# Reading the moving operand of every MLP product in another order: pairs of four-element groups, taken in turn

## The chip, the cores and the metric

The kernel runs on one core of a Trainium2 chip. The metric is the device time of one execution in microseconds (us). Engines: PE is TensorE (matmuls; PEld is its weight load), DVE is VectorE, ACT is ScalarE, POOL is GpSimd, SP is SyncE, which issues most DMAs.

## What is computed

A chunked state-space scan over 4 sequences of 768 tokens and 8 heads, then two MLPs on its 3072 tokens of 256 features:

```python
x = attn_out.transpose(0, 2, 1, 3).reshape(B * S, H * D)      # 3072 x 256
xn = x / sqrt(mean(x * x) + 1e-06) * rms_g
x = (silu(xn @ w_gate) * (xn @ w_val)) @ w_out                # d_ff 1536
h = x @ w_in                                                  # d_ff 2048
out = softplus(h) @ w_out2
```

Nothing mixes tokens after the scan: each token goes through the norm and both MLPs by itself.

## The kernel before

Features lie on the 128 partitions and tokens along the free dimension. The tokens come in 24 units of 128; four units make a block of 512 tokens, and there are six blocks. A unit's scan runs on DVE (L561), its small matmuls on PE, and its norm on PE, DVE, ACT and POOL (L571 to L778). Each fp32 value that goes into an MLP product is split into a high and a low part of type fp32r (`xxh` and `xxl` for an input, `hw` for a hidden step, `..h` and `..l` for weights), and a product of two fp32 matrices is three matmuls: high by high, high weight by low input, low weight by high input.

For layer 1 a block runs 12 steps over the hidden features. A step's front, in `three_pass` (L791 to L797), makes two times six matmuls of 128 x 512 (weights `wg` and `wv`, two halves of the 256 features) into a PSUM tile `p`. ACT applies SiLU, DVE multiplies (L829), and ACT and DVE split the result into `hw` (L353, L360). The step's back (L868 to L873) adds six matmuls with `wo` into two tiles `t`. For layer 2 there are 16 steps with six matmuls of `wi` in front and six of `wp` behind. The two tiles `t` of a finished layer 1 are split again into `xxh` and `xxl` and are the input of layer 2; those of layer 2 are copied and stored to `out_y`, which is features by tokens, and the host transposes it. Every matmul goes through the helper `mm` (L322), so PE's rows in the profile all have line L322 and are told apart by their tiles.

At the start, matmuls of a constant by a constant keep PE busy until the first block is ready (the fillers, `p<-mean`: both operands are a single element, broadcast by a step of zero to 128 x 128 and 128 x 512).

The order of instructions on every engine is made before the launch by the class `Plan`. Each operation has a duration on its engine, a rank and its dependencies; the planner runs a list schedule on these and writes the instructions in the order found. Block 0's preparation has places written by hand. A product's duration and the due times of the steps are in units of `MM`, the time of one column, which stands in one line:

```python
    MM = 0.227 / 512
```

The weights come from HBM in 34 chunks (`wr`, L434) during the first third and are unpacked by two ACT and two DVE instructions each (L442 to L451), so the early blocks are calculated while weights are converted and later units are scanned.

Of the kernel before, what the change touches and what calls it, by code (L numbers as in the profile page):

```python
# [17 lines left out]
P = 128  # L18
NB, NH, SEQ, HD, NS = 4, 8, 768, 32, 16
DM = NH * HD  # L20
UPB = SEQ // P
# [38 lines left out]
KD = DM // P  # L60
# [229 lines left out]
def tile_ssd_then_swiglu_then_softplus_mlp(  # L290
# [17 lines left out]
    def buf(tag, shape, dt=F32, bufs=1):  # L308
        if bufs not in pools:
            pools[bufs] = ctx.enter_context(tc.tile_pool(name=f"sb{bufs}", bufs=bufs))  # L310
        return plan.buf(pools[bufs], bufs, tag, shape, dt)
# [5 lines left out]
    def pbuf(tag, shape):  # L317
        p, n = {"p": (ps_p, 4), "a": (ps_a, 2), "t": (ps_t, 2)}[tag]
        return plan.buf(p, n, tag, shape, F32)

    def mm(o, l, r, start, stop):
        pe.matmul(out=o, lhsT=l, rhs=r, start=start, stop=stop, skip_group_check=True)  # L322

    def f32(t):
        return t.bitcast(F32)

# [3 lines left out]
    def PE(ns, rank, fn, r=(), w=(), cols=0):  # L330
        plan.op({"pe": (ns, fn)}, rank, r, w, cols)
# [10 lines left out]
    def DVE(n, rank, fn, r=(), w=(), fast=False, port=True, ns=None):  # L342
        plan.op({"dve": (ns or dve_ns(n, fast), fn) + (("port",) if port else ())}, rank, r, w)
# [7 lines left out]
    def COPY(n, rank, out, in_, r, w, sbuf=True, on=("act",)):  # L351

        ways = {"act": (act_ns(n), lambda: act.activation(out=out(), in_=in_(), func=ACTF.Copy)),  # L353
                "dve": (dve_ns(n, sbuf), lambda: dve.tensor_copy(out(), in_())) + (("port",) if sbuf else ())}  # L354
        plan.op({e: ways[e] for e in on}, rank, r, w)

    def REST(n, rank, out, in_, hi, r, w, on=("dve",)):

        def fn(eng):
            return lambda: eng.tensor_tensor(out=out(), in0=in_(), in1=f32(hi()), op=ALU.subtract)  # L360
        ways = {"dve": (dve_ns(n), fn(dve), "port"), "pool": (pool_ns(n), fn(pool), "port")}
        plan.op({e: ways[e] for e in on}, rank, r, w)
# [31 lines left out]
        W[nm] = [const.tile([P, n, KD, P], F32R, name=f"{nm}{s}") for s in "hl"]  # L394


    MM = 0.227 / 512
    blocks, u0 = [], 0
    t_nom = T0
    for nu in BLOCKS:  # L400
        blocks.append(dict(u0=u0, nu=nu, n=nu * P, d1=18 * nu * P * MM, d2=12 * nu * P * MM))
        u0 += nu
# [5 lines left out]
    for layer, t in seq:  # L408
        b = blocks[t]
# [11 lines left out]
    def weight(c):  # L421
# [3 lines left out]
        if nm in ("wo", "wp"):  # L425
# [23 lines left out]
        ACT(n, rank, lambda: act.activation(out=h, in_=r(), func=ACTF.Copy, scale=256.0), [raw], [(nm, i, 0)])  # L449
        plan.now = first[3]  # L450
        DVE(n, rank, lambda: dve.scalar_tensor_tensor(out=l, in0=r(), scalar=256.0, in1=f32(h), op0=ALU.mult,  # L451
            op1=ALU.subtract), [raw, (nm, i, 0)], [(nm, i, 1)])
        plan.now = None
# [238 lines left out]
    def norm(t, o0, nu, rank, step, at):  # L692
# [6 lines left out]
        if t > 1:  # L699
# [9 lines left out]
            def msum():  # L709
                for k, p in enumerate((hi, lo)):  # L710
                    mm(nb()[:, 0:nu * P], mean.to_broadcast([P, P]).bitcast(F32R), p(), k == 0, k == 1)
            PE(2 * n * MM * 1e3, rank, msum, [hl, (hl, 1), "mean"], [nb], 2 * n)

# [74 lines left out]
    acc = {}  # L788
    x2 = {}

    def three_pass(o, wt, f, xh, xl, n):  # L791
        for k in range(KD):
            a = W[wt][0][:, f, k]
            b = W[wt][1][:, f, k]
            mm(o, a, xh[:, k, 0:n], k == 0, False)
            mm(o, a, xl[:, k, 0:n], False, False)
            mm(o, b, xh[:, k, 0:n], False, k == KD - 1)  # L797

    def wkeys(wt, f):
        return [(wt, f // 2, 0), (wt, f // 2, 1)]  # L800
# [12 lines left out]
    def front1(t, f, rank, new_table, early=False):  # L813
# [5 lines left out]
        for wt in ("wg", "wv"):  # L819
            gp = pbuf("p", [P, 4 * P])  # L820
            PE(6 * n * MM * 1e3, rank, lambda gp=gp, wt=wt: three_pass(gp()[:, 0:n], wt, f, xh(), xl(), n),
               xk + wkeys(wt, f), [gp], 6 * n)
# [10 lines left out]
    def front2(t, f, rank, new_table):  # L833
        bl = blocks[t]
        n = bl["n"]
        xh, xl = x2[t]
        hp = pbuf("p", [P, 4 * P])
        PE(6 * n * MM * 1e3, rank, lambda: three_pass(hp()[:, 0:n], "wi", f, xh(), xl(), n),
           [(x, m) for x in (xh, xl) for m in range(KD)] + wkeys("wi", f), [hp], 6 * n)
        s = buf("s", [P, 4 * P], F32, N_S)  # L840
        ACT(n, rank - EPI, lambda: act.activation(out=s()[:, 0:n], in_=hp()[:, 0:n], func=ACTF.Softplus), [hp],  # L841
            [s, "table"] if new_table and f == 0 else [s], 1283 if new_table and f == 0 else 0)
        if not (new_table and f == 0):
            plan.readers.setdefault("table", []).append(len(plan.ops) - 1)
        split_h((2, t, f), s, n, rank)

    def back(layer, t, f, rank):
        bl = blocks[t]
        n = bl["n"]
        nf, wt = ((F1, "wo"), (F2, "wp"))[layer - 1]  # L850
        if f == 0:
            acc[t] = [pbuf("t", [P, 4 * P]) for _ in range(KD)]
        hhl = H.pop((layer, t, f))

        end = (layer, t) == seq[-1] and f == nf - 1
        if end:

            def prods(p):
                for m in range(KD):
                    a, b = (W[wt][s][:, f, m] for s in (0, 1))  # L860
                    if p:
                        mm(acc[t][m]()[:, 0:n], a, hhl()[:, 1, 0:n], False, True)
                    else:
                        mm(acc[t][m]()[:, 0:n], a, hhl()[:, 0, 0:n], False, False)
                        mm(acc[t][m]()[:, 0:n], b, hhl()[:, 0, 0:n], False, False)
            for p in range(2):
                PE((4 - 2 * p) * n * MM * 1e3, rank, lambda p=p: prods(p), [hhl] + [(hhl, 1)] * p + wkeys(wt, f), list(acc[t]), (4 - 2 * p) * n)
        for m in range(0 if end else KD):  # L868
            def prod(m=m, o=acc[t][m]):
                a, b = (W[wt][s][:, f, m] for s in (0, 1))  # L870
                mm(o()[:, 0:n], a, hhl()[:, 0, 0:n], f == 0, False)
                mm(o()[:, 0:n], a, hhl()[:, 1, 0:n], False, False)
                mm(o()[:, 0:n], b, hhl()[:, 0, 0:n], False, f == nf - 1)  # L873
            PE(3 * n * MM * 1e3, rank, prod, [hhl, (hhl, 1)] + wkeys(wt, f), [acc[t][m]], 3 * n)
        if f < nf - 1:
            return
        if layer == 1:
            x2[t] = [buf(f"xx{k}", [P, KD, 4 * P], F32R, 3) for k in "hl"]
            for m in range(KD):
                h, l = ((lambda s=s, m=m: x2[t][s]()[:, m, 0:n]) for s in (0, 1))  # L880
                av = lambda a=acc[t][m]: a()[:, 0:n]
                COPY(n, rank - EPI, h, av, [acc[t][m]], [(x2[t][0], m)], False)
                DVE(n, rank - EPI, lambda h=h, l=l, av=av: dve.tensor_tensor(out=l(), in0=av(), in1=f32(h()), op=ALU.subtract),
                    [acc[t][m], (x2[t][0], m)], [(x2[t][1], m)], port=False)
        else:
            for m in range(KD):
                o = buf("s", [P, 4 * P], F32, N_S)
                COPY(n, rank - EPI, lambda o=o: o()[:, 0:n], lambda a=acc[t][m]: a()[:, 0:n], [acc[t][m]], [o], False,
                     ("dve",) if end and m else ("act",))
                c0 = bl["u0"] * P  # L890
                plan.op({"actq" if end and m else "sp": (1024, lambda o=o, m=m, q=act if end and m else nc.sync: q.dma_start(
                    out=out[m, :, c0:c0 + n], in_=o()[:, 0:n]))}, rank, [], [o])
# [117 lines left out]
def _launch(arrays):  # L1010
    import numpy as np
    import concourse.bacc as bacc
    from concourse.bass_utils import run_bass_kernel_spmd

    nc = bacc.Bacc("TRN2", target_bir_lowering=False, num_devices=1, dynamic_dma_scratch_size=1024)
    args, feed = [], {}
    for name, a in arrays.items():
        a = np.ascontiguousarray(a)
        feed[f"in_{name}"] = a
        args.append(nc.dram_tensor(f"in_{name}", a.shape, mybir.dt.from_np(a.dtype), kind="ExternalInput").ap())  # L1020
    args.append(nc.dram_tensor("out_y", (KD, P, NT), F32, kind="ExternalOutput").ap())
    with tile.TileContext(nc) as tc:
        tile_ssd_then_swiglu_then_softplus_mlp(tc, *args)
    return run_bass_kernel_spmd(nc, [feed], core_ids=[0]).results[0]["out_y"]
# [47 lines left out]
```

## Time and profile before

| | |
|---|---|
| median of 3 runs | 629.41 us (627.18 to 630.6) |
| the profiled execution | 629.57 us, of which its span is 627.8 us |
| PE busy | 622.6 us, 99% of the span |
| DVE busy | 351.9 us, 56% |
| ACT busy | 312.3 us, 50% |
| chain that ended last | 97% PE |

The span goes from the first to the last instruction of the program. The trace gives each instruction's start and duration. On PE a matmul starts before the one ahead of it has ended, so that durations overlap and their sum means little: how long one takes from the next is the difference of two start times, divided by the matmuls between. A group's line gives the busy time as the union of its instructions and the mean duration of one. Idle time before an instruction is put down to what released it.

### The profile page before, as it was taken

The numbers are of one execution on the slowest core, as the hardware profiler recorded it, in microseconds if no ns is written. First come the engines' busy times: TensorE is split into PE (matmuls) and PEld (weight loads), VectorE is DVE, ScalarE is ACT, GpSimd is POOL, SyncE is SP. The second block draws the span as 40 slices with busy tenths as digits, with TensorE's granted clock in tenths as the row PEclk, the third lists the DMA queues.
The fourth block names the chain that finished last, engine by engine and source line by source line (L and its number), as shares of the span: only waits on it lengthen the run. The fifth ranks groups of instructions, "written<-read, shape, count | busy, mean of one in ns | idle before, by whom it ended". The sixth has DMA issues, their size and how long they took to land.

```text
span 627.8 us, 8758 instructions
## 1 busy us (share of the span) xinstructions
PE 622.6 (99%) x3377; PEld 511.2 (81%) x3377; DVE 351.9 (56%) x561; ACT 312.3 (50%) x547; POOL 20.1 (3%) x41
## 2 busy tenths in 40 slices
PE   9999999999999999999999999999999999999997
PEld 7877788888888888888888888888888888888885
DVE  6999996788683236694333768645333433322222
ACT  2576665777555435444555344555423323643543
POOL 3310000000000000000000000000000000000000
PEclk9899999999999999999999999999999999999999
DMA  6667667576610014110346432400000000000000
GB/s 204 198 203 262 225 225 200 171 228 214 198 46 34 0 50 162 51 57 20 130 172 199 144 106 60 139 1 0 34 1 1 0 1 2 0 1 0 34 1 33
DMA packets 33433, 59.74 MB, mean 95 GB/s; under 512 B 3120, under 2 KB 14960, under 8 KB 33392
## 3 DMA queue, kind: packets, MB, share of 16 engines
q1 hardware_dynamic: 33248, 58.93, 28.7%
q8 instruction: 26, 0.43, 0.3%
q10 hardware_dynamic: 144, 0.26, 0.1%
q14 instruction: 15, 0.12, 0.1%
HBM read 47.45 MB, written 11.73 MB: 94 GB/s over the span
## 4 chain that ended last, share of the span: by engine, by line
PE 97%; DVE 1%; issue 0%; POOL 0%; ACT 0%; DVEq 0%; ACTq 0%
PE p L322 55%; PE t L322 37%; PE a L322 6%; DVE xxl L561 0%; DVE ab L610 0%; DVE xxh L561 0%; POOL xxl L360 0%; DVE xxl L610 0%; DVE xxh L610 0%; DVE s L354 0%; POOL rs L757 0%; DVE wr L445 0%; DVE xxl L778 0%; ACT xxh L353 0%; ACT wgh L449 0%
## 5 line engine op out<-in xcount | busy, mean ns | idle before, releaser
L360 DVE TENSOR_TENSOR hw<-s,hw 128x512 fp32r<-128x512 f32 x164 | 113.2, 691 | 158.1 <-ACT hw L353 157.3
L353 ACT ACTIVATE hw<-s 128x512 fp32r<-128x512 f32 x164 | 103.4, 632 | 103.6 <-DVE s L829 77.8
L322 PE MATMUL t<-hw,wph 128*128 128x512 f32 x384 | 118.9, 390 | 0.0
L841 ACT ACTIVATE s<-p 128x512 f32<-128x512 f32 x96 | 57.2, 598 | 88.2 <-PE p L322 84.6
L829 DVE TENSOR_TENSOR s<-s,p 128x512 f32<-128x512 f32 x72 | 49.4, 686 | 74.3 <-PE p L322 64.2
L322 PE MATMUL t<-hw,woh 128*128 128x512 f32 x272 | 84.6, 392 | 0.0
L322 PEld LDWEIGHTS t<-hw,wph 128*128 128x128 f32 x384 | 71.7, 188 | 15.6 <-ACT hw L353 0.4
L322 PE MATMUL p<-xxh,wih 128*128 128x512 f32 x192 | 75.0, 391 | 0.0
L322 PE MATMUL t<-hw,wpl 128*128 128x512 f32 x192 | 74.7, 389 | 0.0
L322 PE MATMUL p<-xxl,wih 128*128 128x512 f32 x192 | 74.7, 389 | 0.0
L322 PE MATMUL p<-xxh,wil 128*128 128x512 f32 x192 | 74.7, 389 | 0.0
L825 ACT ACTIVATE s<-p 128x512 f32<-128x512 f32 x72 | 43.0, 598 | 56.2 <-PE p L322 53.8
L322 PEld LDWEIGHTS t<-hw,woh 128*128 128x128 f32 x272 | 50.5, 188 | 11.1 <-issue 0.6
L322 PE MATMUL p<-xxh,wgh 128*128 128x512 f32 x144 | 56.5, 393 | 0.0
L322 PE MATMUL p<-xxh,wvh 128*128 128x512 f32 x144 | 56.3, 391 | 0.0
L322 PE MATMUL p<-xxl,wgh 128*128 128x512 f32 x144 | 56.2, 390 | 0.0
L322 PE MATMUL p<-xxl,wvh 128*128 128x512 f32 x144 | 56.1, 389 | 0.0
L322 PE MATMUL p<-xxh,wgl 128*128 128x512 f32 x144 | 56.1, 389 | 0.0
L322 PE MATMUL p<-xxh,wvl 128*128 128x512 f32 x144 | 56.1, 389 | 0.0
L322 PE MATMUL t<-hw,wol 128*128 128x512 f32 x136 | 53.0, 389 | 0.0
L561 DVE TENSOR_TENSOR_SCAN ab<-ab,ident 128x512 f32<-128x512 f32 x40 | 48.7, 1219 | 0.1
L322 PEld LDWEIGHTS p<-xxh,wih 128*128 128x128 f32 x192 | 36.0, 188 | 7.8 <-issue 0.4
(131 smaller groups left out, 751.7 us busy)
## 6 DMA issues: line engine op xcount, KB each, us to landing
wr<-in_w SPq DMA_DIRECT2D x34, 512.0 KB, 4.6
ab<-a_clip SPq DMA_DIRECT2D x20, 512.0 KB
parts<-wr SPq DMA_DIRECT2D x16, 512.0 KB
xc<-in_xc SPq DMA_DIRECT2D x20, 256.0 KB, 4.6
st<-parts SPq DMA_DIRECT2D x16, 256.0 KB, 4.4
cz<-parts SPq DMA_DIRECT2D x32, 128.0 KB, 2.8
out_y<-s SPq DMA_DIRECT2D x11, 256.0 KB, 3.6
wr<-in_bc SPq DMA_DIRECT2D x8, 256.0 KB, 3.0
```

Source lines behind the costliest of these rows:

```text
L322: pe.matmul(out=o, lhsT=l, rhs=r, start=start, stop=stop, skip_group_check=True)
L353: ways = {"act": (act_ns(n), lambda: act.activation(out=out(), in_=in_(), func=ACTF.Copy)), "dve": (dve_ns(n, sbuf), lambda: dve.tensor_co ...
L360: return lambda: eng.tensor_tensor(out=out(), in0=in_(), in1=f32(hi()), op=ALU.subtract)
L561: DVE(512, rank[0], lambda t=t, d=d: dve.tensor_tensor_scan(out=t(), data0=d(), data1=ident4, initial=0.0, op0=ALU.mult, op1=ALU.add), dk ...
L825: ACT(n, rank - EPI, lambda: act.activation(out=s()[:, 0:n], in_=ps[0]()[:, 0:n], func=ACTF.Silu), [ps[0]], [s, "table"] if new_table else ...
L829: DVE(n, rank - EPI, lambda: dve.tensor_tensor(out=s()[:, 0:n], in0=s()[:, 0:n], in1=ps[1]()[:, 0:n], op=ALU.mult), [s, ps[1]], [s], port= ...
L841: ACT(n, rank - EPI, lambda: act.activation(out=s()[:, 0:n], in_=hp()[:, 0:n], func=ACTF.Softplus), [hp], [s, "table"] if new_table and f ...
```

## The change

A function `swap` reorders the view of the moving operand, and all products of both MLPs read through it. The view cuts the 512 tokens into groups of eight, and each eight into two halves of four elements, and reads the halves in turn: elements 0, 4, 1, 5, 2, 6, 3, 7. The result of the product is written in the order of reading, so a product's output has its tokens exchanged within eight. A token goes through four such products (front and back of two layers); three exchanges give the order back, so the final output stands as after one, which the host undoes with a transpose. The weights, the outputs of the products and all other engines' views are as before.

```diff
+    def swap(t):
+        return t.rearrange("p (g l e) -> p g e l", l=2, e=4)
...
-    MM = 0.227 / 512
+    MM = 0.216 / 512
...
-            mm(o, a, xh[:, k, 0:n], k == 0, False)
-            mm(o, a, xl[:, k, 0:n], False, False)
-            mm(o, b, xh[:, k, 0:n], False, k == KD - 1)
+            mm(o, a, swap(xh[:, k, 0:n]), k == 0, False)
+            mm(o, a, swap(xl[:, k, 0:n]), False, False)
+            mm(o, b, swap(xh[:, k, 0:n]), False, k == KD - 1)
...
-                mm(o()[:, 0:n], a, hhl()[:, 0, 0:n], f == 0, False)
-                mm(o()[:, 0:n], a, hhl()[:, 1, 0:n], False, False)
-                mm(o()[:, 0:n], b, hhl()[:, 0, 0:n], False, f == nf - 1)
+                mm(o()[:, 0:n], a, swap(hhl()[:, 0, 0:n]), f == 0, False)
+                mm(o()[:, 0:n], a, swap(hhl()[:, 1, 0:n]), False, False)
+                mm(o()[:, 0:n], b, swap(hhl()[:, 0, 0:n]), False, f == nf - 1)
...
-    o = o.reshape(DM, UPB, NB, P).transpose(2, 1, 3, 0)
+    o = o.reshape(DM, UPB, NB, P // 8, 4, 2).transpose(2, 1, 3, 5, 4, 0)
```

The three products of the last back step (L861 to L866) are changed in the same way. Since `MM` sets the planner's durations and due times, the order of the instructions moves too. PE's is the same up to the 42nd product. There, in block 0, stand the small matmuls of a unit of block 1 (`a<-xc,Sm`, `a<-xc`, `a<-ab,xc`). Before:

```order
L322 MATMUL a<-xc,Sm 128x128 x2
L322 MATMUL a<-xc 32x64 x4
L322 MATMUL a<-ab,xc 32x128 x8
L322 MATMUL p<-xxh,wgh 128x512
L322 MATMUL p<-xxl,wgh 128x512
L322 MATMUL p<-xxh,wgl 128x512
L322 MATMUL p<-xxh,wgh 128x512
L322 MATMUL p<-xxl,wgh 128x512
L322 MATMUL p<-xxh,wgl 128x512
```

And after:

```order
L322 MATMUL p<-xxh,wgh 128x512
L322 MATMUL p<-xxl,wgh 128x512
L322 MATMUL p<-xxh,wgl 128x512
L322 MATMUL p<-xxh,wgh 128x512
L322 MATMUL p<-xxl,wgh 128x512
L322 MATMUL p<-xxh,wgl 128x512
L322 MATMUL a<-xc,Sm 128x128 x2
L322 MATMUL a<-xc 32x64 x4
L322 MATMUL a<-ab,xc 32x128 x8
```

The unit's matmuls stand six products later.

On PE, at the end of block 0, stands the matmul that broadcasts block 1's norm over the partitions (`a<-ident_68,rs`). Before, it has 180 products ahead of it, and the first product of block 1 is the 211th:

```order
L322 MATMUL a<-ident_68,rs 128x128 x4
L322 MATMUL p<-xxh,wvh 128x512
L322 MATMUL p<-xxl,wvh 128x512
L322 MATMUL p<-xxh,wvl 128x512
L322 MATMUL p<-xxh,wvh 128x512
L322 MATMUL p<-xxl,wvh 128x512
L322 MATMUL p<-xxh,wvl 128x512
L322 MATMUL t<-hw,woh 128x512 x2
L322 MATMUL t<-hw,wol 128x512
L322 MATMUL t<-hw,woh 128x512 x2
L322 MATMUL t<-hw,wol 128x512
```

And after, where it has 192 products ahead of it:

```order
L322 MATMUL p<-xxh,wvh 128x512
L322 MATMUL p<-xxl,wvh 128x512
L322 MATMUL p<-xxh,wvl 128x512
L322 MATMUL p<-xxh,wvh 128x512
L322 MATMUL p<-xxl,wvh 128x512
L322 MATMUL p<-xxh,wvl 128x512
L322 MATMUL t<-hw,woh 128x512 x2
L322 MATMUL t<-hw,wol 128x512
L322 MATMUL t<-hw,woh 128x512 x2
L322 MATMUL t<-hw,wol 128x512
L322 MATMUL a<-ident_68,rs 128x128 x4
```

The broadcast stands 12 products later, and the first product of block 1 is the 211th as before.

On DVE, behind the same norm: multiplies by the broadcast (`xxl<-xxl,a`), the low parts of the split (`xxl<-xxl,xxh`), and between them work on weights (`wol`), on hidden steps (`s`, `hw`) and on a later block's rows (`wr<-wr`). Before:

```order
L778 TENSOR_TENSOR xxl<-xxl,a 128x512
L451 SCALAR_TENSOR_TENSOR wol<-wr,woh 128x512
L829 TENSOR_TENSOR s<-s,p 128x512
L360 TENSOR_TENSOR xxl<-xxl,xxh 128x512
L778 TENSOR_TENSOR xxl<-xxl,a 128x512
L360 TENSOR_TENSOR hw<-s,hw 128x512
L482 TENSOR_TENSOR wr<-wr 128x512
L360 TENSOR_TENSOR xxl<-xxl,xxh 128x512
```

And after (the lines are five higher):

```order
L783 TENSOR_TENSOR xxl<-xxl,a 128x512 x2
L365 TENSOR_TENSOR hw<-s,hw 128x512
L365 TENSOR_TENSOR xxl<-xxl,xxh 128x512
L487 TENSOR_TENSOR wr<-wr 128x512
L834 TENSOR_TENSOR s<-s,p 128x512
L365 TENSOR_TENSOR xxl<-xxl,xxh 128x512
```

From the first multiply to the last split there were eight instructions, and there are seven now.

## Rows read from the trace of the kernel before

**Rows 1.** The page: busy time by engine, and the chain that ended last.

```profile
PE 622.6 (99%) x3377; PEld 511.2 (81%) x3377; DVE 351.9 (56%) x561; ACT 312.3 (50%) x547; POOL 20.1 (3%) x41
...
PE 97%; DVE 1%; issue 0%; POOL 0%; ACT 0%; DVEq 0%; ACTq 0%
```

**Rows 2.** Waits of PE: who waited for whom, total us, times, longest us.

```profile
PE p L322 <- DVE small L945: 0.9, 1, 0.9
PE p L322 <- POOL rs L757: 0.2, 1, 0.2
```

**Rows 3.** Timeline of PE at 304 us: start us, us, engine, instruction, count.

```profile
304.24 0.39 PE L322 MATMUL p<-xxh,wih 128*128 128x512 f32 x1
304.47 0.39 PE L322 MATMUL p<-xxl,wih 128*128 128x512 f32 x1
...
305.60 0.62 PE L322 MATMUL t<-hw,wph 128*128 128x512 f32 x2
306.05 0.39 PE L322 MATMUL t<-hw,wpl 128*128 128x512 f32 x1
...
308.32 0.39 PE L322 MATMUL p<-xxh,wih 128*128 128x512 f32 x1
```

**Rows 4.** Busy time in stretches: engines, granted clock, DMA share and GB/s.

```profile
core 0: us, PE busy (x) PEld busy (x) DVE busy (x) ACT busy (x) POOL busy (x), PEclk, DMA share, GB/s
8.20:10.30 2.10, 2.10 (x13) 1.88 (x12) 2.10 (x3) 0.00 (x0) 1.33 (x3) 1.00 0.89 254
28.00:29.30 1.30, 1.30 (x5) 1.03 (x4) 1.30 (x4) 0.66 (x2) 0.00 (x0) 0.50 0.20 39
30.00:90.00 60.00, 60.00 (x392) 47.61 (x391) 57.74 (x104) 38.54 (x74) 3.73 (x4) 1.00 0.66 223
260.00:280.00 20.00, 20.00 (x90) 16.50 (x89) 17.05 (x26) 9.37 (x18) 0.00 (x0) 1.00 0.19 69
460.00:580.00 120.00, 120.00 (x531) 99.34 (x531) 39.70 (x58) 45.57 (x74) 0.00 (x0) 1.00 0.00 1
```

**Rows 5.** A PE group of the page: instructions, busy us, mean ns, idle.

```profile
L322 PE MATMUL p<-xxh,wih 128*128 128x512 f32 x192 | 75.0, 391 | 0.0
```

**Rows 6.** Durations min/median/max ns: fillers from 8 us, products from 460 us.

```profile
L322 PEld LDWEIGHTS p<-mean x10: 187/188/191, 8.1 to 10.4; 128*128 128x128 f32 x10
L322 PE MATMUL p<-mean x9: 378/381/382, 8.2 to 10.4; 128*128 128x512 f32 x9
...
L322 PEld LDWEIGHTS t<-hw,wph x62: 187/188/188, 542.8 to 579.7; 128*128 128x128 f32 x62
L322 PE MATMUL t<-hw,wph x62: 389/389/389, 543.0 to 580.0; 128*128 128x512 f32 x62
```

**Rows 7.** Timeline of PE at 9 us, four fillers between unit matmuls.

```profile
9.34 1.03 PE L322 MATMUL p<-mean 128*128 128x512 f32 x4
10.21 0.40 PE L322 MATMUL p<-st,small 128*128 128x256 f32 x2
```

**Rows 8.** Timeline of PE at 28 us: three fillers, and the next.

```profile
27.81 1.49 PE L322 MATMUL p<-mean 128*128 128x512 f32 x3
...
29.09 0.63 PE L322 MATMUL p<-mean 128*128 128x512 f32 x1
```

**Rows 9.** Timelines of PE and DVE, 80 to 90 us: block 1's norm.

```profile
81.75 1.05 PE L322 MATMUL a<-ident,rs 128*128 128x128 f32 x8
82.56 0.48 PE L322 MATMUL p<-xxh,wvh 128*128 128x512 f32 x1
...
89.48 0.39 PE L322 MATMUL p<-xxh,wgh 128*128 128x512 f32 x1
...
83.02 0.68 DVE L778 TENSOR_TENSOR xxl<-xxl,a 128x512 f32<-128x512 f32 x1
...
87.24 0.69 DVE L360 TENSOR_TENSOR xxl<-xxl,xxh 128x512 fp32r<-128x512 f32 x1
```

More of the change, by code (lines that the diff above doesn't have):

```diff
@@ L861, in prods @@
                     if p:
-                        mm(acc[t][m]()[:, 0:n], a, hhl()[:, 1, 0:n], False, True)
+                        mm(acc[t][m]()[:, 0:n], a, swap(hhl()[:, 1, 0:n]), False, True)
                     else:
-                        mm(acc[t][m]()[:, 0:n], a, hhl()[:, 0, 0:n], False, False)
-                        mm(acc[t][m]()[:, 0:n], b, hhl()[:, 0, 0:n], False, False)
+                        mm(acc[t][m]()[:, 0:n], a, swap(hhl()[:, 0, 0:n]), False, False)
+                        mm(acc[t][m]()[:, 0:n], b, swap(hhl()[:, 0, 0:n]), False, False)
             for p in range(2):
```

## The prediction

> **What bounds the kernel now.** I first read the share of busy time and the chain that ended last: TensorE (PE) has 622.6 us of a span of 627.8, and 97% of the chain is PE [rows 1]. A busy PE alone does not say that PE is the bound, because the ends of its matmuls are modelled, so I looked next at what PE waited for: 0.9 us at the start and 0.2 us once, nothing else [rows 2]. So from the first product to the last PE runs from one matmul to the next, and what sets the time is the pace of those matmuls.
>
> The pace is read from the start times, not from the durations, which overlap. Between 304.24 and 308.32 us stand 18 products (the 6 of one `wi` step, then 12 of two pairs of `wp` steps): 4.08 us / 18 = 226.7 ns each [rows 3]. The stretch from 460 to 580 us confirms it over a longer way: 531 matmuls touch 120 us, two of which began before, so 120 / 529 = 226.8 ns [rows 4]. There are 6 blocks of 12 x 18 + 16 x 12 products, 2448 in all, of which the group of the `wi` products shows its 6 x 16 x 2 = 192 [rows 5]. 2448 x 226.7 ns = 555 us: the change touches 88% of the span.
>
> Why 226.7? [...] Other engines and DMA: from 460 to 580 us DMA moves 1 GB/s and VectorE (DVE) is busy a third of the time, and the pace is no better than at 304 us, where weights and units still come in [rows 3, 4]. The weight load: 188 ns for a product's and 188 ns for a filler's, alike [rows 6]. The moving operand: the fillers at the head are matmuls of the same shape and type whose moving operand is one element read 512 times, and four of them take 10.21 - 9.34 = 0.87 us, 217.5 ns each, while DVE is busy throughout and DMA moves 254 GB/s [rows 4, 7]. Their median duration is shorter by the same kind of step, 381 against 389 ns [rows 6]. So what a product pays over a filler, about 9 ns, goes with walking through 512 elements, and that walk is the one thing that the change alters in each product.
>
> [...]
>
> **The change part by part.** *The new read order* (all 2448 products). It adds and removes no instruction. Within each eight neighbours the columns go in as 0, 4, 1, 5, 2, 6, 3, 7, so each group of four is still used up once and within eight columns. [...] No effect: 226.7 ns, nothing. A loss: the rivals below have it. [...] The filler shows what a product costs when the walk is free, so I take a value between the floor and the filler, 216 ns: 2448 x (226.7 - 216) = 26.2 us. With the filler's 217.5 it would be 22.5 us.
>
> [...]
>
> *The planner's constant.* `MM` goes from 0.227 to 0.216 per 512 columns, so due times move and the order on every engine changes; the numbers of instructions on PE, DVE, ScalarE (ACT), POOL and the load queue stay the same, and up to the 42nd product so does PE's order. It is an input, and says nothing on the chip. Its cost sits where another engine has no room. From 30 to 90 us DVE is busy 57.74 of 60 us [rows 4], and in it lies the norm of block 1, whose result the first product of block 1 (the 211th in program order) reads. Before: broadcast on PE at 81.75, multiplies from 83.02, last split at 87.24 + 0.69 = 87.93, first use at 89.48 [rows 9]; that is 6.18 us of chain and 1.55 us to spare. After: the broadcast stands 12 products later, with 18 products left to the first use. These and the broadcast itself (82.56 - 81.75 = 0.81 us) last 18 x 0.216 + 0.81 = 4.7 us. If the chain takes 6.18 us as before, PE waits 1.5 us; with one DVE instruction fewer between first multiply and last split (about 0.6 us), 0.8 us. If DVE paces all of block 0, PE wins nothing on its 210 products, 210 x 10.7 ns = 2.2 us lost; if the cover holds, 0. I take 1.2 us. The next fullest place, 260 to 280 us, has DVE at 17.05 of 20 us [rows 4], and 17.05 / 19.1 still leaves a tenth free: nothing.
>
> *The output's order* is set right on the host by a transpose of the result, outside the time. The output of each product is still written to consecutive places, and ACT, DVE and the DMAs see the same shapes as before: nothing.
>
> **Sum.** The profiled execution took 629.57 us, of which 627.8 are span; the median of the runs is 629.41, the same within 0.03%. 629.57 - 26.2 + 1.2 = 604.6 us.
>
> **The rivals.** (a) *The walk costs by bytes, whatever the order.* [...] Against it: nothing in the rows but that today's reads leave one group of four and need the next at once, which the new order spreads. Then only the plan changes, 629.6 to 631 us with the wait of 0 to 1.5 us at block 1.
>
> (b) *Slower: each change of group is paid.* The old order leaves a group of four 127 times in a product, the new one 511 times. [...]
> [...]
>
> (c) *Half the gain.* The extra cycles fall only in part, to some 221 ns: 2448 x 5.7 ns = 14 us, less the 1.2, 616.8 us.
>
> **How the numbers follow.** Forecast, products at the pace of a free walk: 0.74, with its own range from 597 (floor, no wait) to 610 us (filler's pace and 2.2 us lost). (c), 610 to 622: 0.08. (a), 627 to 631: 0.08. (b), 700 and up: 0.10. A measurement of this kernel tells about 0.5%, 3 us, from no change. Faster by more than that are the forecast and (c), 0.82; within it (a), 0.08; slower (b), 0.10. The forecast and (c) hold 0.82, so the range goes from 597 to 620 us, and the other two stay outside.
>
> **What would show it.** In the trace after, 18 products between the same places should take 3.89 us in place of 4.08, in the quiet stretch after 440 us as well as in the busy one; the duration recorded of one should fall from 389 toward 381 ns, and the weight loads stay at 188. PE should show a wait of about a microsecond on DVE or ACT at the 211th product and next to none elsewhere, DVE should be as long busy as now, 352 us, in a shorter span. I am wrong if products keep 226.7 ns (a), if they take 260 ns and more (b), or if the pace falls but PE's waits in the first 100 us exceed 2.2 us.

## The result, and the profile after

The changed kernel took 603.77 us (median of 4 runs, 601.38 to 604.33) beside 629.5 us before: ratio 0.9589, 95% interval 0.9551 to 0.9626. The prediction was 604.6 us. The profiled execution took 604.33 us with a span of 601.3 us. A row of the profile after whose line number is five higher than before is the same code, since `swap` added five lines.

Busy time by engine and the chain that ended last, of the kernel after (beside [rows 1]), and PE's waits (beside [rows 2]):

```profile
PE 595.0 (99%) x3377; PEld 513.7 (85%) x3377; DVE 351.2 (58%) x561; ACT 309.5 (51%) x547; POOL 20.0 (3%) x41
...
PE 94%; DVE 3%; DMA 1%; issue 0%; ACT 0%; POOL 0%; DVEq 0%; ACTq 0%
```

```profile
PE p L322 <- DVE small L950: 0.9, 1, 0.9
PE t L322 <- DVE hw L365: 0.9, 2, 0.7
PE p L322 <- POOL rs L762: 0.2, 1, 0.2
```

The other engines do what they did: DVE 351.2 us after 351.9, ACT 309.5 after 312.3. PE still has the chain, and its waits grew by 0.9 us of idle time. The pace is read as in [rows 3], on PE's timeline between two like places (start us, us, instruction, count):

```profile
291.46 0.38 PE L322 MATMUL p<-xxh,wih 128*128 128x512 f32 x1
291.68 0.38 PE L322 MATMUL p<-xxl,wih 128*128 128x512 f32 x1
...
292.76 0.59 PE L322 MATMUL t<-hw,wph 128*128 128x512 f32 x2
...
295.35 0.38 PE L322 MATMUL p<-xxh,wih 128*128 128x512 f32 x1
```

18 products take 3.89 us, 216.1 ns each, where they took 4.08. In the quiet stretch of the kernel after, where DMA moves almost nothing (columns as in [rows 4]), with the durations (min/median/max ns) of its weight loads and products beside those of [rows 6]:

```profile
435.00:555.00 120.00, 120.00 (x557) 105.08 (x557) 41.74 (x61) 47.54 (x78) 0.00 (x0) 1.00 0.00 1
...
L322 PEld LDWEIGHTS t<-hw,wph x60: 189/189/189, 520.1 to 553.3; 128*128 128x128 f32 x60
L322 PE MATMUL t<-hw,wph x60: 379/379/379, 520.3 to 553.5; 128*128 128x512 f32 x60
```

557 matmuls touch 120 us, two of them begun before: 216.2 ns. The duration fell from 389 to 379 ns, the weight load stayed. All of the 2448 products that follow one another undisturbed go at this pace; over all start times the median is 216 ns, and the mean of the undisturbed ones is 215.8.

Where the 26.5 us of span come from: the first product starts at 30.03 us (30.51 before), and from there to the end it is 571.27 us (597.29 before), 26.0 us less. 2448 x (226.7 - 215.8) ns is 26.7 us. That the sum comes out lower has two parts of opposite sign, which are taken up below: new waits, and products just behind other matmuls that no longer lose time.

### The profile page after: what moved, and what is told of

The parts are those of the page before. It is cut to its first block, busy times and chain, and to the rows that moved or that the text cites. A ratio compares the mean times of both kernels' runs of the same rounds, so it can differ in the third digit from the quotient of the medians.

```text
span 601.3 us, 8773 instructions
## 1 busy us (share of the span) xinstructions
PE 595.0 (99%) x3377; PEld 513.7 (85%) x3377; DVE 351.2 (58%) x561; ACT 309.5 (51%) x547; POOL 20.0 (3%) x41
## 4 chain that ended last, share of the span: by engine, by line
PE 94%; DVE 3%; DMA 1%; issue 0%; ACT 0%; POOL 0%; DVEq 0%; ACTq 0%
PE p L322 53%; PE t L322 35%; PE a L322 6%; DMA wr<-in_w 1%; DVE hw L365 1%; DVE wr L450 0%; DVE s L834 0%; DVE ab L566 0%; DVE xxl L783 0%; POOL xxl L365 0%; DVE xc L730 0%; DVE xxl L615 0%; DVE wol L456 0%; DVE s L359 0%; DVE wvl L456 0%
## 5 line engine op out<-in xcount | busy, mean ns | idle before, releaser
L322 PE MATMUL t<-hw,wph 128*128 128x512 f32 x384 | 114.7, 380 | 0.1
L322 PE MATMUL t<-hw,woh 128*128 128x512 f32 x272 | 82.3, 383 | 1.0 <-DVE hw L365 0.9
L322 PE MATMUL p<-xxh,wih 128*128 128x512 f32 x192 | 72.8, 379 | 0.0
L322 PE MATMUL p<-xxl,wih 128*128 128x512 f32 x192 | 72.8, 379 | 0.0
L322 PE MATMUL p<-xxh,wil 128*128 128x512 f32 x192 | 72.8, 379 | 0.0
L322 PE MATMUL t<-hw,wpl 128*128 128x512 f32 x192 | 72.8, 379 | 0.0
L322 PE MATMUL p<-xxh,wgh 128*128 128x512 f32 x144 | 55.0, 382 | 0.0
L322 PE MATMUL p<-xxh,wvl 128*128 128x512 f32 x144 | 54.6, 379 | 0.0
L322 PE MATMUL p<-xxl,wgh 128*128 128x512 f32 x144 | 54.6, 379 | 0.0
L322 PEld LDWEIGHTS p<-xxh,wil 128*128 128x128 f32 x192 | 36.3, 189 | 5.1
```

## The experiments

Where kernels are compared closely, the time from the first product to the end is taken, which is called the rest below. It leaves out the start, which varies by itself, as the last section shows.

**The order and the plan apart.** The first kernel keeps the new order and has the old constant, the second has the new constant alone.

```diff
-    MM = 0.216 / 512      # e1_order_old_plan: the changed kernel, but
+    MM = 0.227 / 512
...
-    MM = 0.227 / 512      # e2_new_plan_only: the kernel before, but
+    MM = 0.216 / 512
```

> The new read order with the planner's old constant 0.227, so that the order of instructions is nearly that of before. If the read order alone makes the gain: 18 products in 3.88 us (215.8 ns each), duration 379 ns, about 602 to 606 us; PE's waits in the first 100 us may differ from the 0.4 us of the changed kernel. If the plan carried part of the gain: over 610 us.

> The planner's new constant 0.216 alone, products read in the old order. If the read order alone makes the gain: 226.7 ns a product, 629 to 632 us, no difference that can be measured. If the plan carried part of it: under 626 us.

The order alone: 600.92 us, ratio 0.9558 (0.9528 to 0.9587). The plan alone: 628.75 us, ratio 1.0009 (0.9991 to 1.0027), the same. The quiet stretches of the first and of the second show 215.8 and 226.8 ns (120 us by 556 and 529):

```profile
440.00:560.00 120.00, 120.00 (x558) 105.08 (x557) 40.56 (x60) 49.93 (x83) 0.00 (x0) 1.00 0.01 5
...
460.00:580.00 120.00, 120.00 (x531) 99.41 (x530) 39.67 (x58) 45.57 (x74) 0.00 (x0) 1.00 0.00 1
```

The gain is the order's alone. The rest says what the plan does: 597.29 us before and 598.53 with the new constant; 571.27 us after and 570.47 with the old one. In these profiles the new constant costs about 1 us either way.

**Whose walk costs: the weights' or the moving operand's?** The expectations count in a cycle that is the author's estimate: the 426.7 ns of a filler at a granted 0.50 ([rows 4, 8]), halved for 1.00, are 213.3 ns, a 512th of that is called a cycle, and the 226.7 ns of a product are 32 of these more than 213.3. No run shows such a cycle, or a product at 213.3 ns: the fastest pace of any run is 215.8. A weight load reads 128 elements, which are 32 groups of four as well; so the weight load that runs beside each product was a candidate that its 188 ns in [rows 6] do not rule out. Two kernels replace one of the operands by a single element per partition, as the fillers have both.

```diff
-            a = W[wt][0][:, f, k]                            # e3_flat_weights (all products alike)
+            a = W[wt][0][:, f, k, 0:1].to_broadcast([P, P])
...
     def swap(t):                                             # e4_flat_moving (old constant)
-        return t.rearrange("p (g l e) -> p g e l", l=2, e=4)
+        return t[:, 0:1].to_broadcast([P, 4 * P])
```

> The kernel before with the weights of every product replaced by one of their columns, broadcast, so that a weight load reads one element 128 times; the moving operand is read in the old order. This changes the output. A weight load has 128 elements, 32 groups of four, and the product has 32 cycles too many. If each group of a weight load takes a cycle from the moving read: 216 ns a product, about 603 us. If the moving operand's walk alone costs: 226.7 ns still, about 629 us.

> The kernel before with the moving operand of every product replaced by its first column, broadcast, as the fillers have it; the weights are read as before. This changes the output. If the moving operand's walk costs the 32 cycles: 215.5 to 217.5 ns a product, about 603 us. If the weight load's walk costs them: 226.7 ns and 629 us.

Flat weights, then flat moving operand, quiet stretches:

```profile
460.00:580.00 120.00, 120.00 (x520) 97.82 (x519) 38.78 (x57) 44.41 (x73) 0.00 (x0) 1.00 0.00 1
...
440.00:560.00 120.00, 120.00 (x557) 105.05 (x556) 40.78 (x60) 49.85 (x82) 0.00 (x0) 1.00 0.01 5
```

With a flat moving operand a product takes 216.2 ns (120 us by 555), and the kernel 601.4 us: the walk of the moving operand is the cost, and the new order is as good as no walk at all. With flat weights it is not 216 ns, and not 226.7 either but 231.7 (120 us by 518; 635.37 us). This fits neither of the two outcomes that were expected. So the weight load does not cause what a product takes beyond 216 ns, as e4 shows with the weights read as before, but where it reads does bear on the walk, with 231.7 ns for 226.7; why is open.

The changed kernel has a control of its own. The sums of the norm (`a<-ab,mean`) have the same shape and type, broadcast weights as in e3, and still read their operand in running order. PE's timeline of the kernel after:

```profile
161.90 0.38 PE L322 MATMUL t<-hw,wpl 128*128 128x512 f32 x1
162.12 0.63 PE L322 MATMUL a<-ab,mean 128*128 128x512 f32 x2
162.58 0.59 PE L322 MATMUL t<-hw,wph 128*128 128x512 f32 x2
163.01 0.38 PE L322 MATMUL t<-hw,wpl 128*128 128x512 f32 x1
```

Two of them take 0.46 us, 230 ns each and close to the 231.7 ns of e3, in the midst of products at 0.43 us for two.

**What in the order does it?** Six kernels are the changed one with another `l` and `e` in `swap` (and the host's inverse of it). Each alters all 2448 products and ran once. e5 has a view of the same form as the change, with other numbers in it.

```diff
-        return t.rearrange("p (g l e) -> p g e l", l=2, e=4)     # 0 4 1 5 2 6 3 7
+        return t.rearrange("p (g l e) -> p g e l", l=2, e=2)     # e5_within_group: 0 2 1 3
+        return t.rearrange("p (g l e) -> p g e l", l=4, e=4)     # e6_four_groups: 0 4 8 12 1 5 9 13
+        return t.rearrange("p (g l e) -> p g e l", l=2, e=8)     # e7_groups_apart: 0 8 1 9 2 10
+        return t.rearrange("p (g l e) -> p g e l", l=128, e=4)   # e8_new_group_each: 0 4 8 12 16
+        return t.rearrange("p (g l e) -> p g e l", l=2, e=256)   # e9_halves_apart: 0 256 1 257
+        return t.rearrange("p (g l e) -> p g e l", l=4, e=2)     # e10_two_at_a_time: 0 2 4 6 1 3 5 7
```

> The changed kernel with pairs of two in place of four (columns 0, 2, 1, 3): the order is new, but each group of four is still read to its end before the next. If what helps is to take two groups of four in turn: 226.7 ns a product, about 629 us. If any order other than the running one helps: 216 ns, about 603 us.

> The changed kernel with four groups of four in turn (0, 4, 8, 12, 1, 5, ...). If the read can hold two groups only and pays each change beyond them: over 226.7 ns, up to 267 ns (728 us). If taking groups in turn is free as such: 215.8 ns, about 603 us.

> The changed kernel with two runs of eight in turn (0, 8, 1, 9, ... 7, 15): two groups are held at a time as in the change, but they are not neighbours. If two groups in turn suffice: 215.8 ns, about 603 us. If they must be neighbours: 226.7 ns, about 629 us.

> The changed kernel with all 128 groups of four in turn (0, 4, 8, ..., 508, 1, 5, ...): each read goes to another group, and none is used again before 128 columns. [...] If each change of group that was not read shortly before is paid with a cycle or more, up to one column in two cycles: 267 to 427 ns a product, 728 to 1120 us. If not even that is paid: 215.8 to 226.7 ns, 603 to 629 us.

> The changed kernel with the two halves of the operand in turn (0, 256, 1, 257, ...): two groups of four at a time, 1024 bytes apart. If two groups in turn are free wherever they lie: 215.8 ns a product and 571 to 572 us from the first product to the end. If they must lie close together: over 226.7 ns, up to the 268 ns of four groups in turn.

The expectation of the sixth kernel describes its order wrongly: it is 0, 2, 4, 6, 1, 3, 5, 7, two reads of one group and two of the next, but the two are not neighbours.

> The changed kernel with two neighbouring elements at a time of two groups in turn (0, 1, 4, 5 written the other way round: 0, 2, 4, 6, 1, 3, 5, 7), so each group is read twice, left for two columns, and read twice again. If what helps is that a new group is needed some columns after the group before it was opened, and not four in a row from one: 215.8 ns. If the group must change at each column: 226.7 ns.

Quiet stretches of 120 us in the order e5, e7, e9, e6, e10, e8:

```profile
460.00:580.00 120.00, 120.00 (x531) 99.36 (x530) 39.02 (x57) 46.00 (x75) 0.00 (x0) 1.00 0.00 1
...
440.00:560.00 120.00, 120.00 (x557) 105.08 (x557) 40.88 (x60) 49.86 (x82) 0.00 (x0) 1.00 0.01 5
...
440.00:560.00 120.00, 120.00 (x558) 105.08 (x557) 41.50 (x61) 47.86 (x78) 0.00 (x0) 1.00 0.00 1
...
560.00:680.00 120.00, 120.00 (x448) 84.92 (x447) 32.79 (x48) 42.52 (x70) 0.00 (x0) 1.00 0.01 5
...
700.00:820.00 120.00, 120.00 (x354) 69.54 (x353) 25.39 (x37) 31.72 (x51) 0.00 (x0) 1.00 0.00 0
...
1000.00:1120.00 120.00, 120.00 (x261) 54.18 (x260) 17.12 (x25) 29.00 (x47) 0.00 (x0) 1.00 0.01 5
```

In all six PE is busy for the whole stretch, the granted clock is 1.00 and DMA still; only the count of matmuls differs. With the pace from start times and each kernel's time:

| order of reading | ns a product | us | reads in a row from one group, by every second column |
|---|---|---|---|
| one element only (e4) | 216 | 601.4 | all |
| 0 4 1 5 2 6 3 7 (the change) | 216 | 603.8 | 4 |
| 0 8 1 9 2 10 (e7) | 216 | 602.8 | 4 |
| 0 256 1 257 (e9) | 216 | 608.4 | 4 |
| 0 1 2 3 (before) | 226.7 | 629.5 | 2 |
| 0 2 1 3 (e5) | 227 | 628.5 | 2 |
| 0 4 8 12 1 5 9 13 (e6) | 268 | 730.6 | 1 |
| 0 2 4 6 1 3 5 7 (e10) | 340 | 903.7 | 1 |
| 0 4 8 12 16 (e8) | 461 | 1198.4 | 1 |

e8 and e10 are dearer than any outcome that was expected of them (up to 427 and 226.7 ns). Three explanations fall. That any order but the running one helps, or the form of the view as such: e5 shows no gain. That groups must be neighbours: e7 and e9 go at the same pace, with elements eight and 256 places apart in turn. That the read keeps the last two groups, whichever column asks: then e10, which never has more than two groups in use, would be cheap, and it costs 340 ns. What fits all nine is the count in the last column. Number the columns in the order of reading, take columns 0, 2, 4, ... by themselves and columns 1, 3, 5, ... by themselves, and count how many in a row come from one group of four. Where it is four or more, a product took 216 ns; where it is two, 226.7 and 227; where it is one, 268 to 461. The count was formed on these rows and no further run tested it; what in the read makes it so, no run shows. It does not say why the three orders with single reads differ among themselves, nor why flat weights made the running order dearer.

The halves (e9) are a warning beside it. The pace is the same, yet the rest took 576.1 us for 571.3. In this execution PE's waits came to 3.2 us in eight, seven of them for DVE, beside 2.0 us in four in the kernel after, and from 30 to 90 us PE was busy for 58.95 us beside 59.76. The waits are 1.2 of the 4.8 us more; where the others went is open. DVE's weight conversions from 30 to 200 us took longer there than in the kernel after, and than in the twelve other profiles, which have 683 to 695 ns (the kernel after, then e9; the second number is the mean ns of one):

```profile
L450 DVE SCALAR_TENSOR_TENSOR wr<-wr,zz 128x512 int32<-128x512 int32 x31 | 21.2, 686 | 0.0
L448 DVE SCALAR_TENSOR_TENSOR wr<-wr,zz 128x512 int32<-128x512 int32 x31 | 25.6, 827 | 0.1
```

One execution does not tell whether the order caused that.

**The two plans again, side by side.**

> The changed kernel as it is, beside the next one on the same chip: 600 to 604 us, 571.3 us from the first product to the end.

> The new read order with the planner's constant at 0.227 again. From the first product to the end it took 570.5 us where the changed kernel took 571.3, because PE waits less. If that repeats, the time is 0.5 to 1.5 us under that of the changed kernel, about 0.1 to 0.2%, less than the start varies by; if the 600.9 us seen first were due to the plan, it is 2 to 3 us under.

The changed kernel: 602.12 us (601.77 to 602.56), ratio 0.9582 (0.9565 to 0.9599). With the old constant: 600.97 us (600.48 to 602.26), ratio 0.9568 (0.9549 to 0.9588). The medians differ by 1.15 us and the rest by 1.35 (571.83 and 570.48), as expected; the intervals of the ratios overlap, so as a time the gain of the old constant is not established. The two profiles of the changed kernel differ in the rest by 0.56 us by themselves. The waits of PE in the one and the other tell the same, the two waits for `hw` being there with the new constant alone:

```profile
PE t L322 <- DVE hw L365: 0.9, 2, 0.7
PE p L322 <- DVE small L950: 0.9, 1, 0.9
PE p L322 <- POOL rs L762: 0.2, 1, 0.2
...
PE p L322 <- DVE small L950: 0.9, 1, 0.9
PE p L322 <- POOL rs L762: 0.2, 1, 0.2
PE a L322 <- DVE xxh L739: 0.2, 1, 0.2
```

## Why the prediction was right, point by point

**The bound.** That the pace of PE sets the time was right: with every product 10.9 ns shorter, the rest shrank by 26.0 us, 97% of 2448 x 10.9 ns.

**The candidates.** Other engines and DMA were ruled out from rows, with a granted clock of 1.00 both at the fillers from 8 us and from 460 to 580 us ([rows 4]), and the moving operand's walk was named; e4 shows it. The step was thinner than it read, though: the fillers have no walk in either operand, so equal durations of weight loads did not yet excuse the weights. It took e3 and e4 for that.

**216 ns.** Measured 215.8. It was chosen between the floor of 213.3 and the filler's 217.5, and no row spoke for 216 within them; the filler's own 217.5 was 1.7 ns too high. The floor, which the sum and the range use, is an estimate, half of what a filler took at a granted 0.50 ([rows 4, 8]); no run shows it, and in its place the runs show 215.8 to 216.2 ns for every order at the faster pace. That the choice came so close was luck, though any value between them would have given a gain of 22 us or more.

**Why the order helps.** The verdict was right and its ground incomplete. What the prediction held against (a) was that today's reads leave one group of four for the next at once, which the new order spreads. This is the step that failed, since spreading is not enough: four groups in turn cost 268 ns, and e10, which has two groups in use and no more, costs 340. By the last column of the table, what the orders at 216 ns share is that every second column stays in its group for four reads or more; no run tested that as the cause.

**The wait of 1.2 us.** Right in size by luck, wrong in place. Block 1's norm, on which it was laid, held nothing up. PE's and DVE's timelines of the kernel after at the place of [rows 9]:

```profile
81.51 1.05 PE L322 MATMUL a<-ident,rs 128*128 128x128 f32 x8
...
86.29 0.38 PE L322 MATMUL p<-xxh,wgh 128*128 128x512 f32 x1
...
87.15 0.38 PE L322 MATMUL p<-xxl,wgh 128*128 128x512 f32 x1
87.37 0.38 PE L322 MATMUL p<-xxh,wgl 128*128 128x512 f32 x1
87.58 0.38 PE L322 MATMUL t<-hw,woh 128*128 128x512 f32 x1
88.20 0.48 PE L322 MATMUL t<-hw,woh 128*128 128x512 f32 x1 [0.24 <-DVE hw L365]
88.52 0.38 PE L322 MATMUL t<-hw,wol 128*128 128x512 f32 x1
...
82.66 1.28 DVE L783 TENSOR_TENSOR xxl<-xxl,a 128x512 f32<-128x512 f32 x2
...
86.26 0.68 DVE L365 TENSOR_TENSOR xxl<-xxl,xxh 128x512 fp32r<-128x512 f32 x1
86.86 0.68 DVE L450 SCALAR_TENSOR_TENSOR wr<-wr,zz 128x512 int32<-128x512 int32 x1
87.47 0.68 DVE L365 TENSOR_TENSOR hw<-s,hw 128x512 fp32r<-128x512 f32 x1
```

From the broadcast at 81.51 us to the first product of block 1 at 86.29 us are 4.78 us, as the prediction had them (4.7). The chain from the broadcast to the end of the last split, at 86.26 + 0.68 = 86.94, is 5.43 us, so by the prediction's reckoning PE would have waited 0.65 us. It did not: the first product reads the first half of the features only, and the low part of the second is not read before the fifth product, at 87.15. The failed step is that the chain was taken to end where the first product begins. What did wait stands a little further on: the second product of a back step, for the low part of `hw` that DVE made behind a weight conversion. It starts 0.62 us after the product before it, 0.40 late, and the next one comes 0.32 us after it, 0.10 late. The other wait was not foreseen at all:

```profile
371.72 0.48 PE L322 MATMUL t<-hw,woh 128*128 128x512 f32 x1
372.86 0.48 PE L322 MATMUL t<-hw,woh 128*128 128x512 f32 x1 [0.66 <-DVE hw L365]
```

That is 1.14 us from start to start, 0.92 late, and it belongs to the plan and not to the pace. The kernel with the new constant alone has it at the old pace, on its own timeline:

```profile
386.75 0.49 PE L322 MATMUL t<-hw,woh 128*128 128x512 f32 x1
387.89 0.50 PE L322 MATMUL t<-hw,woh 128*128 128x512 f32 x1 [0.65 <-DVE hw L360]
```

0.40 + 0.92 = 1.3 us, and 1.5 with the late products behind both, beside the 1.2 of the sum. That the lead of the fullest stretch would be eaten up was a reasonable fear. Of the next fullest place, 260 to 280 us, the prediction expected nothing, and it looked no further; the larger wait is at 372 us.

**The sum.** That the profiled execution came within 0.3 us of 604.6 is partly luck as well. The 1.3 us that products behind other matmuls gave back (last section) were not in the sum, the waits were elsewhere, and this execution had 3.0 us outside its span (604.33 - 601.3) where the one before had 1.8.

**The rivals.** (a), a cost by bytes, falls with the change, e7 and e9, which read the same bytes at 216 ns. (b), each change of group paid, was put at 260 ns and more; the 267 ns and 728 us in the expectation of e6 are the author's estimate, which takes the 13.4 ns over the floor four times, for 511 changes of group in place of 127, and rests on that floor. The change does not show it, nor do e7 and e9, which also change group at each column and take 216 ns. Four groups in turn do, with 268 ns and 730.6 us, which may be chance, since the other single-read orders cost 340 and 461. (c), half the gain, has no order near 221 ns.

## What to carry to other kernels

When matmuls stand back to back, take the pace from start times and hold it against a matmul of the same shape that walks through nothing; a gap between the two was here the moving operand's read, and its order can be changed in the view alone wherever what comes later can bear the exchanged columns. For fp32r operands of 512 columns, as here, reading two places in turn took 216 ns for places 4, 8 and 256 elements apart, beside 226.7 in running order; four places in turn (e6) took 268 ns and the steps of two or four elements in e10 and e8 340 and 461. Nothing here says how other types or widths behave. A planner's constant that follows the new pace is no gain by itself: here two waits, 0.40 and 0.92 us, came onto the path with it.

## What was not expected of the hardware

**Products just behind a disturbance.** In the kernel before, the first products behind other matmuls took 229 to 240 ns before they settled at 226.7; by start times there are some 220 such intervals, worth 1.3 us. PE's timeline before and after, at the first products:

```profile
30.51 0.40 PE L322 MATMUL p<-xxh,wgh 128*128 128x512 f32 x1
30.74 0.40 PE L322 MATMUL p<-xxl,wgh 128*128 128x512 f32 x1
30.98 0.40 PE L322 MATMUL p<-xxh,wgl 128*128 128x512 f32 x1
...
30.03 0.38 PE L322 MATMUL p<-xxh,wgh 128*128 128x512 f32 x1
30.25 0.38 PE L322 MATMUL p<-xxl,wgh 128*128 128x512 f32 x1
30.46 0.38 PE L322 MATMUL p<-xxh,wgl 128*128 128x512 f32 x1
```

0.23 and 0.24 us from start to start before, 0.22 and 0.21 after: with the new order they are gone. This 1.3 us nearly paid for the 1.5 us of the waits: 26.7 + 1.3 - 1.5 = 26.5 us, beside 26.0 measured from the first product on; where the other 0.5 us went is open.

**The start.** The first product came between 27.95 and 30.51 us in the profiles of these kernels, whatever the change. The kernel after in its two profiles, 26 to 30 us, has a granted clock of 0.59 and of 1.00:

```profile
26.00:30.00 4.00, 4.00 (x12) 3.37 (x13) 3.18 (x7) 1.75 (x3) 0.00 (x0) 0.59 0.38 119
...
26.00:30.00 4.00, 4.00 (x27) 3.50 (x24) 3.71 (x7) 2.27 (x5) 0.26 (x1) 1.00 0.33 111
```

In the 6 us before, with small matmuls and fillers and short idle times between them, PE was busy for 5.77 us in the first profile, and for 5.78 us in that of e1, which has 1.00 from 26 to 30 us, so how busy it was there does not tell the two apart. In the first profile the granted clock was 0.50 from 26 to 29 us, 0.74 from there to 29.5 and 1.00 to 30, with 12 matmuls for 27, and the first product came at 30.03 us; in the second, at 1.00 from 26 to 30 us, it came at 28.95. The four profiles with a granted clock of 0.57 to 0.61 from 26 to 30 us (before, after, e6, e9) have the first product at 30.03 to 30.51 us, the ten with 1.00 at 27.95 to 29.05.

The start is most of what the spans of one kernel differ by. The new order with the old constant (e1 and e12) has spans of 598.4 and 599.4 us, with the first product at 27.95 and 28.89 us and a rest of 570.47 and 570.48 us. The time outside the span varies as well: in the four runs of the kernel after it is 1.8 to 3.6 us.
